# GLU stage of a training step: tile LayerNorms one iteration later, tile 1 transposed by TensorE, w_down's transposes copied by halves

## The chip, the cores and the metric

One NeuronCore of a Trainium2 chip runs the whole program in one launch. The metric is device time in microseconds (us) of one execution, the median of several runs. A profiled execution gives, besides its time, a trace of every instruction. Engines: PE is TensorE, PEld its weight load, DVE VectorE, ACT ScalarE, POOL GpSimd, SP SyncE, which here only issues DMAs.

## The reference

The kernel computes a transformer block with modulation from a condition vector c, and the gradients of its eleven inputs: `x` (2048 rows of 512), a memory of 8 rows, Wq, Wk, Wv, Wo (32 heads of 128), w_gate, w_up (512 x 1792), w_down (1792 x 512), c and w_mod. All inputs and outputs are bf16. The changed part is the GLU half:

```python
h = _layernorm(x, axis=-1) * (1 + ca) + sa
x = x + ga * _A_ref(h, A_mem0, A_Wq, A_Wk, A_Wv, A_Wo, A_seg_len)   # recurrent attention, 64 segments of 32 rows
h = _layernorm(x, axis=-1) * (1 + cb) + sb
g = jnp.einsum('bsd,df->bsf', h, w_gate)
u = jnp.einsum('bsd,df->bsf', h, w_up)
x = x + gb * jnp.einsum('bsf,fd->bsd', _sigmoid(g) * u, w_down)
```

with `_vjp(grad_out)` of all of it after that.

## The kernel before

The program has four big stages: the attention forward (`phase2`, one iteration for each of 64 segments), the GLU forward and backward (`phase3`), the attention backward, and the remaining weight gradients. The change is in `phase3`, and in one line of `phase2`'s last segment.

`phase3` works through 16 tiles j of 128 rows in a software pipeline of seven steps (`run_pipeline`, L2100). In iteration it, step k works on tile it - k, and the deepest step comes first: s6, s5, ..., s0, and then `after(it)`. The steps are:

- s0 (L1141): issues the loads of tile j+1 on SP (`glu_load`, L1066: x, four DMAs from AOA, dout) and does the LayerNorm of tile j: t0 and x1 (L1150, L1152), statistics on DVE (L1154 to L1158), rstd on POOL (L1161), xhf on DVE (L1165), xh2, a bf16 copy of xhf, on ACT (L1166), h2a and h2 (L1168, L1170) and db = dout * gb (L1173) on DVE; h2 and db are stored from POOL (L1171, L1174). For tile 0 all of this was done within the attention stage.
- s1 (L1178): hdT, the transposes of h2 and db, by two DMA transposes issued by SP (L1183, L1184). Tile 0 has its hdT already.
- s2 (L1194): gate and up on PE, four chunks of 448 columns, alternately (L1205, L1209), with eight evictions on ACT: sg = sigmoid(gate) (L1206) and u (L1210, through the helper at L61). It appends `out`, which makes hh and umh on DVE (L1213, L1215), to the list `late`.
- s3 (L1221): hhT by a DMA transpose (L1225); dU = (db w_down^T) * sg: PE with w_downT (L1232), eviction with the product on DVE (L1234); then `flush()` runs what is in `late`, and dg on DVE (L1236).
- s4 (L1242): the product with w_down (L1247), duT and dgT by DMA transposes (L1250, L1251), b_bf on ACT (L1253).
- s5 (L1266): dh (L1272) with w_upT and w_gateT, and the LayerNorm's backward on DVE and ACT.
- s6 (L1313): sums of rows by PE (L1315), the transpose of da (L1319).

So in a steady iteration PE runs s6, s5, s4, s3, s2 without a break, and the LayerNorm of tile `it` follows the DVE work of s5 and s3.

The weights have to be transposed once: w_downT (`wdT_piece`, L1120: for each of four column blocks c two groups of seven PE transposes into the PSUM tile tp, the first group copied by DVE, the second by ACT), and w_gateT, w_upT (`wT_piece`, L1107, groups of eight, copied by ACT). `turns` (L1130) says in which iteration's `after` they run: w_downT and the first two groups of w_gate in iteration 2, the rest in 3 and 4. The tp tiles have two buffers (`psT`, L1090) and the mm tiles of all products five (`psM`, L1089). hdT, h2, db and sg have two buffers each; u, umh, hhT, duT and dgT one.

The order of instructions on each engine comes from a scheduler, with parts pinned to the program's order: PE and ACT up to the end of iteration 2 (L1352), DVE over the stage (L1374). Each engine then executes its queue strictly in that order, and a waiting instruction holds all behind it. That holds for SP and its DMAs too. A DMA also waits for the landing of the eighth DMA before it on its issuer, whose semaphore it uses again.

In the last attention segment `turn_p` (L872) transposes ET on PE and writes Pst: a copy of 32 rows (L874) and a product with rden (L875), both on DVE, three times.

Of the kernel before, what the change touches and what calls it, by code (L numbers as in the profile page):

```python
# [9 lines left out]
AF = mybir.ActivationFunctionType  # L10
# [30 lines left out]
class K:  # L41
# [395 lines left out]
    def phase2(self):  # L437
        nc, tc, cfg, io = self.nc, self.tc, self.cfg, self.io
        D, DC, H, E, L, M, T, G, NS = cfg.D, cfg.DC, cfg.H, cfg.E, cfg.L, cfg.M, cfg.T, cfg.G, cfg.NS
        GW = 128  # L440
        NP = 3
        PG = 4
# [10 lines left out]
        with ExitStack() as ctx:  # L453
# [39 lines left out]
            NT = cfg.NT  # L493
# [148 lines left out]
            first = b_pieces(0)  # L642
# [160 lines left out]
            for s in range(NS):  # L803
                s4 = s % nseg_t
# [66 lines left out]

                def turn_p(pi):  # L872
                    ps, n = transposes_part(ET, pi)
                    nc.vector.tensor_copy(Pst[96:128, pi * PG:pi * PG + n, :], ps[96:128])  # L874
                    nc.vector.tensor_tensor(Pst[0:120, pi * PG:pi * PG + n, :], ps[0:120],  # L875
                                            rden[:, pi * PG:pi * PG + n].unsqueeze(2).to_broadcast([120, n, 128]), op=ALU.mult)

# [79 lines left out]
                Pst = sb2.tile([128, G, 128], BF16, name="Pst", bufs=1)  # L957
# [119 lines left out]
    def phase3(self):  # L1077
        nc, tc, cfg, io = self.nc, self.tc, self.cfg, self.io
        D, DC, F, FC, NT, T = cfg.D, cfg.DC, cfg.F, cfg.FC, cfg.NT, cfg.T
# [7 lines left out]
        with ExitStack() as ctx:  # L1087
# [5 lines left out]
            w_gate, w_up, w_down, w_gateT, w_upT = self.w_gate, self.w_up, self.w_down, self.w_gateT, self.w_upT  # L1093
            w_downT = wtp.tile([128, DC, F], BF16, name="w_downT")
# [6 lines left out]
            def tp8():  # L1101
                return psT.tile([128, 8, 128], BF16, name="tp", tag="t")
# [4 lines left out]
            def wT_piece(src, dst, fc0, n, k):  # L1107
                def f():
                    for fc in range(fc0, fc0 + n, 2):
                        m = min(2, fc0 + n - fc)  # L1110
                        tp = tp8()
                        for i in range(m):
                            for c in range(DC):
                                nc.tensor.transpose(tp[:, i * DC + c, :], src[:, c, (fc + i) * 128:(fc + i + 1) * 128],
                                                    self.ident[:])
                        self.evac("act" if k is None or (fc // 2 + k) % 2 else "dve", dst[:, fc:fc + m, :],
                                  tp[:, 0:m * DC, :].rearrange("p (i c) d -> p i (c d)", i=m))
                return f

            def wdT_piece(c):  # L1120
                def f():
                    for f0 in range(0, FC, 7):
                        tp = tp8()
                        for i in range(7):
                            nc.tensor.transpose(tp[:, i, :], w_down[:, f0 + i, c * 128:(c + 1) * 128], self.ident[:])
                        self.evac("act" if f0 else "dve", w_downT[:, c, f0 * 128:(f0 + 7) * 128],
                                  tp[:, 0:7, :].rearrange("p i f -> p (i f)"))
                return f

            turns = {2: [wdT_piece(c) for c in range(DC)] + [wT_piece(w_gate, w_gateT, 0, 4, None)],  # L1130
                     3: [wT_piece(w_gate, w_gateT, 4, 10, None), wT_piece(w_up, w_upT, 0, 4, None)],
                     4: [wT_piece(w_up, w_upT, 4, 10, None)]}

# [2 lines left out]
            def load(j):  # L1136
                if j >= NT or j in ins:
                    return
                ins[j] = self.glu_first.get(j) or self.glu_load(j, nc.sync)

            def s0(j):  # L1141
                r0, r1 = j * 128, (j + 1) * 128
                load(j + 1)
                st = ins.pop(j)
                if j == 0:
                    st.update(x1=self.first_x1, rstd=self.first_st[:, 9:10], xh2=self.first_xh2)
                    return st
                a_rows = st["a_rows"]
                t0 = sbp.tile([128, D], F32, name="t0", tag="f32tmp", bufs=5)
                nc.vector.tensor_tensor(t0[:], a_rows[:], ga_bc[:], op=ALU.mult)  # L1150
                x1 = sbp.tile([128, D], F32, name="x1", bufs=4)
                nc.vector.tensor_tensor(x1[:], t0[:], st["x0"][:], op=ALU.add)  # L1152
                sts = sbp.tile([128, 6], F32, name="st", bufs=2)
                nc.vector.bn_stats(sts[:], x1[:])  # L1154
                mv = sbp.tile([128, 2], F32, name="mv", bufs=2)
                nc.vector.bn_aggr(mv[:], sts[:])
                ve = sbp.tile([128, 1], F32, name="ve3", bufs=2)
                nc.vector.tensor_scalar_add(ve[:], mv[:, 1:2], EPS)  # L1158
                rstd = sbp.tile([128, 1], F32, name="rstd2", bufs=6)
                i0 = len(self.traced())  # L1160
                nc.gpsimd.tensor_tensor(rstd[:], ve[:], mhalf[:], op=ALU.pow)  # L1161
                self.pin(i0, [mybir.EngineType.Pool])
                xh2 = sbp.tile([128, D], BF16, name="xh2", bufs=5)
                xhf = sbp.tile([128, D], F32, name="xhf", tag="f32tmp", bufs=5)
                nc.vector.tensor_scalar(xhf[:], x1[:], mv[:, 0:1], rstd[:, 0:1], op0=ALU.subtract, op1=ALU.mult)  # L1165
                nc.scalar.activation(xh2[:], xhf[:], AF.Copy)  # L1166
                h2a = sbp.tile([128, D], F32, name="h2a", tag="f32tmp", bufs=5)
                nc.vector.tensor_tensor(h2a[:], xhf[:], cb1_bc[:], op=ALU.mult)  # L1168
                h2 = sbp.tile([128, D], BF16, name="h2", bufs=2)
                nc.vector.tensor_tensor(h2[:], h2a[:], sb_bc[:], op=ALU.add)  # L1170
                nc.gpsimd.dma_start(self.H2ROWS[r0:r1, :], h2[:])  # L1171
                db = sbp.tile([128, D], BF16, name="db", bufs=2)
                nc.vector.tensor_tensor(db[:], st["dout"][:], gb_bc[:], op=ALU.mult)  # L1173
                nc.gpsimd.dma_start(self.DBROWS[r0:r1, :], db[:])  # L1174
                st.update(db=db, x1=x1, rstd=rstd, xh2=xh2, h2=h2)
                return st

            def s1(j, st):  # L1178
                if j == 0:
                    st["hdT"] = self.first_hdT  # L1180
                    return st
                hdT = sbp.tile([128, 2 * DC, 128], BF16, name="hdT", bufs=2)
                nc.sync.dma_start(hdT[:, 0:DC, :], st["h2"][:], transpose=True)  # L1183
                nc.sync.dma_start(hdT[:, DC:2 * DC, :], st["db"][:], transpose=True)  # L1184
                st["hdT"] = hdT
                return st
# [7 lines left out]
            def s2(j, st):  # L1194
                r0, r1 = j * 128, (j + 1) * 128
                hdT = st["hdT"]
                sg = sbp.tile([128, F], BF16, name="sg", bufs=2)
                u = sbp.tile([128, F], BF16, name="u", bufs=1)
                hh = sbp.tile([128, F], BF16, name="hh", bufs=2)
                umh = sbp.tile([128, F], BF16, name="umh", bufs=1)  # L1200
                for ch in range(NCH):
                    sl = slice(ch * CH, (ch + 1) * CH)
                    gp = mm()
                    for c in range(DC):
                        nc.tensor.matmul(gp[:, 0:CH], lhsT=hdT[:, c, :], rhs=w_gate[:, c, sl], start=(c == 0), stop=(c == DC - 1))  # L1205
                    nc.scalar.activation(sg[:, sl], gp[:, 0:CH], AF.Sigmoid)  # L1206
                    up = mm()
                    for c in range(DC):
                        nc.tensor.matmul(up[:, 0:CH], lhsT=hdT[:, c, :], rhs=w_up[:, c, sl], start=(c == 0), stop=(c == DC - 1))  # L1209
                    self.evac("act", u[:, sl], up[:, 0:CH])  # L1210

                def out():
                    nc.vector.tensor_tensor(hh[:], sg[:], u[:], op=ALU.mult)  # L1213
                    nc.gpsimd.dma_start(self.HHROWS[r0:r1, :], hh[:])
                    nc.vector.tensor_tensor(umh[:], u[:], hh[:], op=ALU.subtract)  # L1215

                late.append(out)
                st.update(sg=sg, hh=hh, umh=umh)
                return st

            def s3(j, st):  # L1221
# [148 lines left out]
                if it >= 5:  # L1370
                    later(it)

            self.run_pipeline(NT, [s0, s1, s2, s3, s4, s5, s6], deepest_first=True, after=after)
            self.pin(i0, [ET.DVE])  # L1374
            self.pin_behind(i0, self.pinned, [ET.PE, ET.DVE, ET.Activation, ET.Pool, ET.SP])
            accs = self.flat(self.Wk, 2 * DC * F, 2 * D, F32)
# [7 lines left out]
        with ExitStack() as ctx:  # L1384
# [36 lines left out]
            for (rows, outw) in ((self.DGROWS, io["out_7"]), (self.DUROWS, io["out_8"])):  # L1421
                for ch in range(NCH):
                    xr = xrs.pop(0)
                    for c in range(DC):
                        ps = psG.tile([128, CH], F32, name="gps", tag="g")
# [864 lines left out]
```

## Time and profile before

| | us |
|---|---|
| time before, median of three runs (lowest, highest) | 3062.4 (3058.02, 3064.0) |
| profiled execution, own time | 3064.78 |
| its span (mean granted clock of TensorE) | 3063.0 (0.991) |
| PE busy in the span | 2975.5 |
| GLU's first gate matmul starts | 976.89 |
| stretch 976 to 1034: PE busy, granted clock | 46.76 of 58, 0.94 |
| stretch 1034 to 1284: PE busy, granted clock | 250.00 of 250, 1.00 |

Times inside the profile count from the start of the span. A line of the view of waits reads: who waited, for whom, us in total, times, longest. A line of a timeline reads: start, duration, engine, line of the kernel, operation, out<-in, partitions x elements; an x and a number at its end say how many like instructions were merged; in brackets stands the idle time of the engine before it, and what ended it. A line of the windows view gives, for a stretch, its length, the busy time of PE, PEld, DVE, ACT and POOL with the number of instructions, the granted clock of TensorE (1.00 is full), the mean busy share of the DMA engines and GB/s. Some tiles live in memory of the attention weights, whose names the profile shows: Wk is w_gate and w_up (as source), Wq is hdT of tile 0 (under L1205, L1209, L1232) and w_gateT, w_upT, Wv is w_down.

### The profile page before, as it was taken

The numbers are of one execution on the slowest core, as the hardware profiler recorded it, in microseconds if no ns is written. First come the engines' busy times: TensorE is split into PE (matmuls) and PEld (weight loads), VectorE is DVE, ScalarE is ACT, GpSimd is POOL, SyncE is SP. The second block draws the span as 40 slices with busy tenths as digits, with TensorE's granted clock in tenths as the row PEclk, the third lists the DMA queues.
The fourth block names the chain that finished last, engine by engine and source line by source line (L and its number), as shares of the span: only waits on it lengthen the run. The fifth ranks groups of instructions, "written<-read, shape, count | busy, mean of one in ns | idle before, by whom it ended". The sixth has DMA issues, their size and how long they took to land. (4 is left out here: it accounts for less than half of the span.)

```text
span 3063.0 us, 106593 instructions
## 1 busy us (share of the span) xinstructions
PE 2975.5 (97%) x44297; PEld 1859.8 (61%) x44297; DVE 1605.9 (52%) x3744; ACT 1288.2 (42%) x3182; POOL 1220.6 (40%) x2645
## 2 busy tenths in 40 slices
PE   6999999999998999989899999999999999999999
PEld 3666666666665544445567777777777754445454
DVE  5566566656656788732255555555555632322230
ACT  2555565555554533321255555555555520101011
POOL 2555555555554222211344444444444422333321
PEclk8999999999999999999999999999999999999999
DMA  9888888888888899987499999999999997666574
GB/s 307 217 219 209 216 220 205 219 215 210 217 215 265 199 230 229 239 254 246 155 248 248 245 246 243 247 246 253 248 239 248 246 284 265 214 193 220 182 247 140
DMA packets 838567, 703.54 MB, mean 230 GB/s; under 512 B 538722, under 2 KB 711042, under 8 KB 837188
## 3 DMA queue, kind: packets, MB, share of 16 engines
q1 hardware_dynamic: 712916, 486.69, 64.3%
q0 software_dynamic: 54512, 148.63, 15.3%
q10 hardware_dynamic: 70656, 61.41, 6.4%
q8 instruction: 348, 5.70, 0.8%
q14 instruction: 135, 1.11, 0.1%
HBM read 295.19 MB, written 276.35 MB: 187 GB/s over the span
## 5 line engine op out<-in xcount | busy, mean ns | idle before, releaser
L2080 PE MATMUL gps<-rows,hrows 128*128 128x512 bf16 (+2 forms) x2160 | 417.5, 355 | 0.0
L2080 PEld LDWEIGHTS <-hrows 128*128 128x128 bf16 x2160 | 211.3, 98 | 204.5
L63 DVE CAST ot<-gps 128x512 bf16<-128x512 f32 (+3 forms) x76 | 48.2, 634 | 294.7 <-PE gps L2080 208.4
L1786 POOL COPY dOst<-RAd 96x512 bf16<-96x512 bf16 x128 | 75.1, 611 | 307.6 <-DVE RAd L63 307.3
L61 ACT ACTIVATE ot<-gps 128x512 bf16<-128x512 f32 (+3 forms) x75 | 41.3, 551 | 359.9 <-PE gps L2080 214.7
L658 PE MATMUL pass_ps<-Wv,hT 128*32 128x512 bf16 (+2 forms) x2304 | 188.2, 357 | 0.0
L2084 POOL DMA_DIRECT2D out_dram<-ot x108 | 81.4, 753 | 260.3 <-DVE ot L63 132.7
L1034 POOL TENSOR_TENSOR Pst<-Pst,rden 120x1408 bf16<-120x1408 bf16 x63 | 159.8, 2536 | 56.7 <-issue 35.3
L255 PEld LDWEIGHTS <-hT 128*32 128x32 bf16 x4096 | 125.1, 97 | 94.2 <-DMA Wq<-in_A_Wq_dram 4.6
L61 ACT ACTIVATE dVT<-g_ps 128x480 bf16<-128x480 f32 (+1 forms) x192 | 104.7, 545 | 97.8 <-PE g_ps L1742 97.4
L63 DVE CAST Vst<-pass_ps 96x512 bf16<-96x512 f32 x128 | 87.3, 682 | 106.4 <-ACT RBv L61 101.3
L215 PE MATMUL dh_ps<-WvT,dVT 128*32 128x512 bf16 x2048 | 134.3, 382 | 0.1
L2094 PE MATMUL gps5o<-WoT,rows 128*128 128x512 bf16 x592 | 128.4, 379 | 1.8 <-DMA rows<-OSR 1.8
L255 PE MATMUL pass_ps<-Wq,hT 128*32 128x512 bf16 x2048 | 125.6, 383 | 4.5 <-DMA Wq<-in_A_Wq_dram 4.5
L223 PE MATMUL at_ps<-Wo,OT 128*32 128x256 bf16 x4096 | 124.6, 274 | 2.8 <-DMA Wo<-in_A_Wo_dram 2.4
L658 PE MATMUL pass_ps<-Wv,hb 128*32 128x512 bf16 (+2 forms) x636 | 127.2, 345 | 0.0
L255 PE MATMUL pass_ps<-Wk,hT 128*32 128x512 bf16 x2048 | 124.8, 381 | 1.8 <-POOL hT L547 1.1
L255 PE MATMUL pass_ps<-WoT,dyT 128*32 128x256 bf16 (+1 forms) x3072 | 122.7, 308 | 0.9 <-ACT dyT L1860 0.9
L223 PE MATMUL dhq_ps<-WqT,dQT 128*32 128x256 bf16 x4096 | 122.9, 273 | 0.0
L793 POOL DMA_DIRECT2D Vst<-RBv x192 | 99.2, 522 | 58.6 <-ACT ET L840 38.3
L215 PE MATMUL dh_ps<-WkT,dKT 128*32 128x512 bf16 x2048 | 122.3, 380 | 0.0
L223 PEld LDWEIGHTS <-dQT 128*32 128x32 bf16 x4096 | 109.8, 97 | 15.6
(448 smaller groups left out, 7007.5 us busy)
## 6 DMA issues: line engine op xcount, KB each, us to landing
OSR<-Ost SPq DMA_DIRECT2D x64, 352.0 KB
OT<-OT SPq DMA_DIRECT2D x64, 352.0 KB
VT<-VTr SPq DMA_DIRECT2D x64, 352.0 KB
PS<-Pst SPq DMA_DIRECT2D x64, 352.0 KB
OT_l<-OT SPq DMA_DIRECT2D x64, 352.0 KB
Pst_l<-PS SPq DMA_DIRECT2D x64, 352.0 KB
VT_l<-VT SPq DMA_DIRECT2D x64, 352.0 KB
DVR<-rows_x POOLq DMA_DIRECT2D x64, 352.0 KB, 6.2
```

Of the source, the lines that this page charges most:

```text
L61: return nc.scalar.activation(out, in_, AF.Copy)
L63: return nc.vector.tensor_copy(out, in_)
L215: self.nc.tensor.matmul(ps[32 * j:32 * j + 32, :], lhsT=lhsT, rhs=w, start=(n < 4), stop=(n >= total - 4), tile_position=(0, 32 * j))
L223: nc.tensor.matmul(ps[32 * j:32 * j + 32, :], lhsT=x[k], rhs=w[k][:, 256 * d:256 * d + 256], start=(n == 0), stop=(n == total - 1), tile_p ...
L255: self.nc.tensor.matmul(ps[32 * j:32 * j + 32, :], lhsT=lhs(c), rhs=rhs, start=(c == 0), stop=(c == DC - 1), tile_position=(0, 32 * j))
L658: nc.tensor.matmul(ps[32 * j:32 * j + 32, o * E:(o + n) * E], lhsT=lhsT, rhs=wc[:, 3 * a + hl:3 * (a + n - 1) + hl + 1:3, :], start=(c == ...
L793: nc.gpsimd.dma_start(Vst[96 + 8 * j:104 + 8 * j, :], rb[32 * j + o:32 * j + o + 8, :])
L1034: nc.gpsimd.tensor_tensor(Pst[0:120, :, :], Pst[0:120, :, :], rden[:, :].unsqueeze(2).to_broadcast([120, G, 128]), op=ALU.mult)
L1786: nc.gpsimd.tensor_copy(dOst[0:96, 512 * hf:512 * hf + 512], RAd[0:96, 512 * hf:512 * hf + 512])
L2080: nc.tensor.matmul(ps[:, 0:ng * E], lhsT=hrows[:, tp_, c * 128:(c + 1) * 128], rhs=rows[:, tp_, 0:ng * E], start=(tp_ == 0), stop=(tp_ == ...
L2084: nc.gpsimd.dma_start(outw[c * 128:(c + 1) * 128, h0:h0 + 3 * (ng - 1) + 1:3, :], ot[:, 0:ng * E].rearrange("p (h e) -> p h e", e=E))
L2094: nc.tensor.matmul(pss[gg][:], lhsT=src[0][:, src[1], gg * E:(gg + 1) * E], rhs=dyrows[:, tp_, :], start=(tp_ == order[0]), stop=(tp_ == o ...
```

## The change

Five edits:

1. For tiles from 2 on, s0 is run at the start of s1: the LayerNorm of tile j moves from iteration j to iteration j+1. There it comes behind s3 of tile j-2, and its own hdT transposes follow at once. Tiles 0 and 1 stay.
2. Tile 1's xh2 is copied by POOL and not by ACT.
3. Tile 1's hdT is made by eight PE transposes into one tp tile and one ACT copy, and not by two DMA transposes.
4. w_downT's transposes run inside s2 of tile 0 (ahead of s1 in iteration 2), ordered by halves: first the four groups of the first seven chunks, copied by ACT, then the four of the second, copied by DVE.
5. In `turn_p` the copy of 32 rows moves from DVE to ACT.

```diff
                     ps, n = transposes_part(ET, pi)
-                    nc.vector.tensor_copy(Pst[96:128, pi * PG:pi * PG + n, :], ps[96:128])
+                    nc.scalar.activation(Pst[96:128, pi * PG:pi * PG + n, :], ps[96:128], AF.Copy)
...
-            def wdT_piece(c):
-                def f():
-                    for f0 in range(0, FC, 7):
+            def wdT_pieces():
+                for f0 in range(0, FC, 7):
+                    for c in range(DC):
                         tp = tp8()
                         for i in range(7):
                             nc.tensor.transpose(tp[:, i, :], w_down[:, f0 + i, c * 128:(c + 1) * 128], self.ident[:])
-                        self.evac("act" if f0 else "dve", w_downT[:, c, f0 * 128:(f0 + 7) * 128],
+                        self.evac("dve" if f0 else "act", w_downT[:, c, f0 * 128:(f0 + 7) * 128],
                                   tp[:, 0:7, :].rearrange("p i f -> p (i f)"))
-                return f
-
-            turns = {2: [wdT_piece(c) for c in range(DC)] + [wT_piece(w_gate, w_gateT, 0, 4, None)],
+
+            turns = {2: [wT_piece(w_gate, w_gateT, 0, 4, None)],
...
-                nc.scalar.activation(xh2[:], xhf[:], AF.Copy)
+                if j == 1:
+                    nc.gpsimd.tensor_copy(xh2[:], xhf[:])
+                else:
+                    nc.scalar.activation(xh2[:], xhf[:], AF.Copy)
...
                 hdT = sbp.tile([128, 2 * DC, 128], BF16, name="hdT", bufs=2)
+                if j == 1:
+                    tp = tp8()
+                    for i in range(2 * DC):
+                        src = st["h2"] if i < DC else st["db"]
+                        nc.tensor.transpose(tp[:, i, :], src[:, (i % DC) * 128:(i % DC) * 128 + 128], self.ident[:])
+                    nc.scalar.activation(hdT[:], tp[:], AF.Copy)
+                    st["hdT"] = hdT
+                    return st
...
                 st.update(sg=sg, hh=hh, umh=umh)
+                if j == 0:
+                    wdT_pieces()
                 return st
...
-            self.run_pipeline(NT, [s0, s1, s2, s3, s4, s5, s6], deepest_first=True, after=after)
+            first = lambda j: s0(j) if j < 2 else None
+            second = lambda j, st: s1(j, st if j < 2 else s0(j))
+            self.run_pipeline(NT, [first, second, s2, s3, s4, s5, s6], deepest_first=True, after=after)
```

As the scheduler places them, in the changed program: on PE the first three w_down groups follow tile 0's gate and up, and the other five, tile 1's eight transposes and the two first w_gate groups alternate with dU's matmuls of tile 0; on ACT the four w_downT copies follow u of tile 0, then come hdT of tile 1 and two w_gateT copies, and xh2 of tile 2 stands ahead of the last u of tile 1; on SP hhT, duT and dgT of tile 0 come ahead of hdT of tile 2, and in each later iteration hdT comes ahead of duT, dgT and hhT, where it stood behind them.

## The prediction

> **What bounds the kernel now.** I read the page's busy times first, then the PE's waits in the stage that is edited (976 to 1034 us of the span), then its windows, then the timelines of ACT and PE there.
>
> ```profile
> PE 2975.5 (97%) x44297; PEld 1859.8 (61%) x44297; DVE 1605.9 (52%) x3744; ACT 1288.2 (42%) x3182; POOL 1220.6 (40%) x2645
> ```
>
> PE is busy for 97% of the span: time is won only where PE waits or runs slowly. The view of who waited for whom, for PE from 976 to 1034 us, lists us in total, times, longest:
>
> ```profile
> PE mm L1209 <- ACT sg L1206: 4.2, 1, 4.2
> PE mm L1247 <- DMA hhT<-hh: 2.0, 1, 2.0
> PE tp L1114 <- ACT Wq L61: 1.9, 1, 1.9
> PE tp L1125 <- ACT w_downT L61: 1.7, 1, 1.7
> PE tp L1125 <- DVE w_downT L63: 0.6, 1, 0.6
> ```
>
> The windows view (PE, PEld, DVE, ACT, POOL busy; granted clock; DMA share; GB/s) shows a second loss, the clock:
>
> ```profile
> 981.80:985.20 3.40, 0.15 (x1) 0.10 (x1) 2.50 (x6) 1.27 (x3) 1.18 (x3) 1.00 0.65 189
> 985.20:988.60 3.40, 3.40 (x10) 1.37 (x9) 2.88 (x6) 2.45 (x6) 1.14 (x2) 0.50 0.57 174
> 988.60:992.00 3.40, 1.67 (x23) 1.35 (x22) 2.62 (x6) 2.05 (x4) 0.66 (x2) 1.00 0.56 150
> 1005.70:1009.10 3.40, 1.44 (x18) 0.91 (x16) 3.33 (x5) 2.87 (x5) 1.65 (x3) 1.00 1.05 267
> 1009.10:1012.50 3.40, 3.40 (x24) 2.28 (x22) 0.29 (x1) 1.88 (x2) 0.00 (x1) 0.50 1.16 134
> 1028.00:1284.00 256.00, 255.76 (x1344) 123.48 (x1344) 210.45 (x384) 101.20 (x175) 61.98 (x114) 1.00 0.95 223
> ```
>
> Twice a stretch with little PE work is followed by 3.4 us at half clock. The last row is the steady loop: PE has no gap at all, so nothing can be won there, only lost. All the gain has to come from the ramp before 1028. Where the 4.2 us come from stands in ACT's timeline (start, us, ..., idle before):
>
> ```profile
> 983.93 0.63 ACT L1166 ACTIVATE xh<-xhf 128x512 bf16<-128x512 f32 x1 [9.70 <-DVE xhf L1165]
> 984.47 0.53 ACT L1206 ACTIVATE sg<-mm 128x448 bf16<-128x448 f32 x1
> 984.89 0.54 ACT L61 ACTIVATE u<-mm 128x448 bf16<-128x448 f32 x1
> ```
>
> xh of tile 1 stands ahead of tile 0's first sigmoid on ACT and waits for DVE's LayerNorm. PE fills its five buffers and stops. PE's timeline gives the marks that I sum between:
>
> ```profile
> 985.05 1.55 PE L1209 MATMUL mm<-Wk,Wq 128*128 128x448 bf16 x4 [4.21 <-ACT sg L1206]
> 989.00 0.94 PE L1125 MATMUL tp<-ident,Wv 128*128 128x128 bf16 x14
> 999.23 0.92 PE L1205 MATMUL mm<-Wk,hdT 128*128 128x448 bf16 x4
> 1008.30 0.82 PE L1247 MATMUL mm<-Wv,hhT 128*128 128x512 bf16 x3 [1.96 <-DMA hhT<-hh]
> 1015.40 3.19 PE L1232 MATMUL mm<-w_downT,hdT 128*128 128x448 bf16 x16
> ```
>
> **Part 1: xh of tile 1 goes to POOL; ACT is free for the sigmoids.** Removed from ACT: one copy of 0.63 us with its 9.70 us of idle. What is late next? The built program keeps the old waits of the first sg and the first u: they write memory that the last attention segment's VTr and Ost held, so they wait for the stores VT<-VTr (issued 974.63) and OSR<-Ost (976.06). The trace has these landing at 980.84 and 981.96, long before 984.47, so they were hidden. Now they are the bound. I take sg at 980.95 and u at 982.05. After u, ACT issues one eviction per 0.43 us (984.47 to 984.89). PE's group of four costs 0.757 (977.65 to 978.40). PE's fifth group ends at 980.7 at the latest; the sixth needs sg's buffer (981.55 to 982.3), the seventh u's (982.65 to 983.4), the eighth ends at 984.2. Before, the w_down turns began at 989.00: **4.8 us earlier**. Of that 2.5 to 2.9 is the earlier ACT, the rest the half clock (groups of 1.55 and 1.70 us instead of 0.92).
>
> The clock: a 1.44 us busy window was followed by 0.50, one of 1.67 by 1.00. The new window 978.4 to 981.8 holds some 2.4 us of PE work. I take no slow window; bound 0 to 1.7 us (half of 3.4). The Trainium skill, "TensorE: Matmul & The Clock Gate", Part 1, puts half rate after at least one idle window of about 3.4 us; by it the sum would be the same, but the row of 1.44 us shows that a window need not be empty, and the measurement decides.
>
> On POOL the copy costs about 0.62 (its 128x512 copies of L752 at 970.07), at 983.9, ahead of the store of h2, which waits until 985.35 anyway: nothing. The Trainium skill, "GPSIMD Engine Reference", Key points, speaks against this: POOL shares its SBUF interfaces with VectorE and contends with DVE instructions of two SBUF inputs, and h2a at 983.93 is one. If both stretched, LayerNorm of tile 1 would end later than 985.96, yet DVE is first needed at 988.2 (below): 2.2 us of cover, so zero by either.
>
> **Part 2: LayerNorm of tile 2 leaves the ramp; w_down by halves.** Nine DVE instructions (986.37 to 992.2) stood before DVE's w_downT copies, and ACT's second xh (990.18) before ACT's. Both go. The order is now four copies on ACT (0.92 each, one per 0.83 back to back), then four on DVE (0.62). With two tp buffers, I go through PE's new order: tp1, tp2 by 985.0; ACT copies 985.05 to 988.5 behind the last u; tp3 when tp1 is out (986.0), tp4 986.9, tp5 987.7, tp6 988.55, tp7 and tp8 989.0 to 990.15 against DVE's copies 988.2 to 990.85; dU's matmuls of tile 0 fit in the gaps. Part 3 adds eight transposes of tile 1 (0.45 us, as L1114's eight at 997.46 to 997.90) and one ACT copy 128x1024 of 1.0 us, in place of two DMA transposes: PE 990.35, ACT 990.9 to 991.9; the two w_gate turns, the last four dU matmuls, and tile 1's gate starts at 993.2. This stretch lasts 9.0 us against 10.2 (989.00 to 999.23): **1.2 us**. Without the free DVE, tp5 to tp8 would cost it back.
>
> **Part 3: to dU of tile 1 (before 999.23 to 1015.40, 16.2 us).** Gate and up of tile 1 take 6.05, to 999.25. hhT of tile 0 waited behind two hdT transposes and the loads (issued 1001.01, landed 1008.25). Now it has no transposes ahead and hh is ready at 992.0: issue about 993.6, landing 4 to 7.2 us later, at most 1000.8; PE wants it at 1000.2 and can use it until 1001.5. That wait goes, and the second half-clock window with it. What is late next is ACT: xh of tile 2 now lies on it behind DVE (hh, umh 2.2, du 2.3, dg 1.1, LayerNorm to xhf 3.8 from 990.85: 1000.1), then u, then seven copies of w_gate and w_up of 0.93: the last tp is free at 1005.7, dU of tile 1 starts at 1006.9. 13.7 us: **2.5 us**.
>
> hdT of tile 2 is now behind duT and dgT of tile 0 on SP (4.1 and 3.8 us of issue, rows at 1003.54 and 1007.75): issue 1004.3 to 1007.0, landing 2.6 to 4 us later, 1008 to 1011; PE wants it at 1009.9. Up to a microsecond late, but the next wait of 1.9 us (L1114 for ACT, itself set by DVE) hides that. I take nothing, bound 0 to 1.5.
>
> **Part 4: all later tiles.** DVE's order is unchanged but for the tile's number, and SP's transposes move: hdT of a tile now waits for the LayerNorm of the same iteration, and duT, dgT and hhT stand behind it. Steady iteration at 1066.20: db is written at 1070.15, gate and up of that hdT start at 1078.87, 8.7 us. Issue 1.3 and 1.3 to 2.5, landing 2.6 to 6.9 us after issue in all rows: early enough by 1 to 5 us. duT (issued 1069.99, used at 1085.6), dgT (1073.01, 1088.6) and hhT (1076.61, 1091.6) slip by 2.6 us and have 9 and more to spare after landing. In tile 15 the LayerNorm moves to 1252 to 1259, where DVE idled 2.5 and 4.3 us; its hdT is needed at 1266.9. Nothing. The loads of x, AOA and dout go one iteration later together with their tile, so their lead stays one iteration of 18.8 us, and they land 2 to 5 us after issue. POOL's stores of h2 and db of tile 15 end by 1262; they are read back into memory that holds w_gate until 1273.
>
> **Part 5: three Pst copies to ACT.** DVE loses 0.43, 0.43, 0.36; ACT takes about 0.5 each (128x480 at 966.44: 0.47) in its idle 1.84 before 973.64. ao_b_lo then comes 0.6 earlier and so does PE's first gate, which then waits for the stores all the same: nothing; at most 0.5 lost.
>
> **Sum:** 4.8 + 1.2 + 2.5 = 8.5 us. The profiled execution took 3064.8 (span 3063.0): 3056.3. It lies 2.4 above the median of 3062.4, so 3053.9 for a median. About 0.2% (6 us) is what a measurement here can tell from no change.
>
> **Rivals.** A, the stores: VT and OSR took 6.2 and 5.9 us to land, but the QST stores just ahead in their queue 12.6 and 13.4. If the two land 3 us later, or a window falls to half clock after all, part 1 keeps 1 to 2 us, and all 4.5: 3058. For it: DMA share near 1.0 up to 981.8. Against: neither is touched by the change. B, SP's queue: hhT or hdT of tile 2 late by 3 us or more, since transposes took 4 us each in the ramp: gain 5, 3057.5. C, slower: the steady loop gets a wait for hdT. It decides from 8.7 us after db; beyond that each microsecond is paid by 13 tiles. One microsecond: 13 - 8.5 = 4.5 slower, 3067; two, 3080. For it: rows of 6.1 to 6.9 us behind hhT, plus issue of 2.5. Against: hdT now goes out before the other transposes, into the emptiest part of the iteration.
>
> **Chances.** Forecast 0.62; A 0.19; B 0.11; C 0.08. A and B lie mostly within 0.2% (0.26 of their 0.30), the forecast a little (0.02 of it): faster 0.64, within 0.2% 0.28, slower 0.08. Range 3050.5 to 3061: parts 1 to 3 with 2.5 more at best, A and B with their bounds at worst; C is left out.
>
> **What would show it.** Right: PE's wait for sg under 1.6 us and sg at 981; no window at 0.50 before 990; tile 1's gate at 992 to 994; dU of tile 1 at 1006 to 1008; no PE wait for hhT; no gap in the steady loop. Wrong: any PE wait for hdT, sg later than 982.5, or duT or dgT that PE waits for.

## The result, and the profile after

| | before | changed |
|---|---|---|
| median of 22 runs each, us (lowest, highest) | 3059.94 (3053.95, 3064.86) | 3054.16 (3046.44, 3060.67) |
| profiled execution: span, us | 3063.0 | 3050.6 |

The ratio is 0.9981, with an interval of 0.9973 to 0.9988: faster by 3.7 to 8.3 us, 5.8 by the medians, which is 0.19% and clear of no change. A second comparison (8 runs of the changed kernel, 12 of before) gave 0.9974 (0.9964 to 0.9985).

The two spans differ by 12.4 us, more than the medians do, so the first thing is to locate that. I take the same matmuls in both traces, counted from the first gate matmul of the stage (976.89 before, 977.98 after). A second profile of the changed kernel stands beside the first; "sg" is ACT's first sigmoid, "w_down's turns" are the PE transposes of w_down, "acc" is the first L1315 matmul of a tile (L1327 after); with that of tile 0 the steady loop begins, and what lies ahead of it I call the ramp.

| us from the first gate matmul | before | changed | changed, 2nd profile |
|---|---|---|---|
| first sg | 7.58 | 4.25 | 4.99 |
| w_down's turns start | 12.11 | 7.47 | 8.19 |
| gate of tile 1 | 22.34 | 16.58 | 17.30 |
| dU of tile 1 | 38.51 | 30.17 | 34.63 |
| gate of tile 2 | 41.54 | 35.72 | 37.66 |
| acc of tile 0 | 70.51 | 64.68 | 65.87 |
| from there to acc of tile 12 | 225.65 | 225.65 | 225.65 |

So the ramp became 5.8 us shorter (4.6 in the second profile), about as much as the medians differ by; the steady loop is the same to 0.01 us. Of the 12.4 us, minus 1.1 lies ahead of the stage, 5.8 in the ramp, 0.1 from tile 12 to 15 and 7.6 behind the stage's last acc, where both kernels have the same instructions in the same order on every engine. From that acc to the end the changed kernel's two profiles took 1738.0 and 1738.3 us, the kernel before 1745.6, and the other eleven profiles below 1737.3 to 1743.5. The longest of the eleven is e7, the kernel before with one edit, so these profiles do not exclude an effect of the change behind the stage; in the 240 us behind that acc the granted clock is 0.95 in both of these and 0.97 in the changed kernel. I still take most of the 7.6 us for scatter of single executions, because the profiled executions lie apart by that much: that of the kernel before took 3064.78 us, 4.8 above its median, that of the changed kernel 3052.34, 1.8 below its own. That is argued and not shown; the interval of the gain leaves room for some us outside the ramp.

Now the ramp. PE's waits from 977 to 1034 in the changed kernel (the four largest; who waited for whom, us in total, times, longest):

```profile
PE mm L1215 <- DMA hdT<-h: 2.4, 1, 2.4
PE tp L1125 <- ACT w_downT L61: 1.0, 1, 1.0
PE mm L1219 <- ACT sg L1216: 0.9, 1, 0.9
PE tp L1114 <- ACT Wq L61: 0.7, 2, 0.5
```

The 4.2 us for sg are down to 0.9, those for hhT and most of those for ACT are gone; a wait for hdT, which before did not have, is the largest. ACT's timeline shows that the first sg and u are now held by the landing of the stores, as forecast (OSR landed at 983.24; the releaser named for sg is the one the profile infers, VT<-VTr landed at 982.13). In all seven profiles where the first sg comes behind that landing (this one, e1, e7, e8, e10, e11, e12) it starts 0.10 to 0.11 us after it:

```profile
982.23 0.54 ACT L1216 ACTIVATE sg<-mm 128x448 bf16<-128x448 f32 x1 [6.22 <-DMA AOA<-at_rb]
983.34 0.54 ACT L61 ACTIVATE u<-mm 128x448 bf16<-128x448 f32 x1 [0.57 <-DMA OSR<-Ost]
```

PE's timeline has the marks, and the gap of 2.36 us at 1013.70 with matmuls of 1.70 us behind it:

```profile
985.45 0.94 PE L1125 MATMUL tp<-ident,Wv 128*128 128x128 bf16 x14
...
994.56 0.92 PE L1215 MATMUL mm<-Wk,hdT 128*128 128x448 bf16 x4
...
1001.82 1.04 PE L1259 MATMUL mm<-Wv,hhT 128*128 128x512 bf16 x3 [0.15 <-DMA hhT<-hh]
...
1008.15 3.19 PE L1244 MATMUL mm<-w_downT,hdT 128*128 128x448 bf16 x16
1013.70 1.07 PE L1215 MATMUL mm<-Wk,hdT 128*128 128x448 bf16 x4 [2.36 <-DMA hdT<-h]
1014.57 1.70 PE L1219 MATMUL mm<-Wk,hdT 128*128 128x448 bf16 x4
```

The windows view says why they are slow: the window with the wait (1.04 us of PE work) is followed by one at 0.50. The window that I had feared, at 980, stayed at full clock.

```profile
980.20:983.60 3.40, 2.50 (x14) 1.17 (x12) 2.41 (x5) 0.80 (x2) 2.07 (x5) 1.00 1.06 396
...
1011.00:1014.40 3.40, 1.04 (x6) 0.41 (x5) 3.23 (x6) 0.00 (x0) 1.08 (x2) 0.99 1.22 135
1014.40:1017.80 3.40, 3.40 (x11) 1.32 (x9) 2.58 (x6) 1.09 (x3) 1.10 (x2) 0.50 1.06 363
```

And SP's queue (start, us that the issue took) shows what hdT of tile 2 stood behind. h was ready at 1002.79, db at 1003.39; the transpose of h went out at 1007.74 and landed at 1013.65, just ahead of the gate that needs it, that of db went out at 1009.35 and landed at 1014.15:

```profile
995.90 1.96 SPq L1237 DMA_TRANSPOSE hhT<-hh  x1
997.97 4.10 SPq L1262 DMA_TRANSPOSE duT<-du  x1
1002.16 4.17 SPq L1263 DMA_TRANSPOSE dgT<-dg  x1
1006.43 1.22 SPq L1071 DMA_DIRECT2D Wv<-in_A_x_dram  x1
1007.74 1.51 SPq L1193 DMA_TRANSPOSE hdT<-h  x1
1009.35 1.53 SPq L1194 DMA_TRANSPOSE hdT<-db  x1
```

### The profile page after: what moved, and what is told of

It is laid out like the page before. It is cut to its first block, busy times and chain, and to the rows that moved or that the text cites. A ratio compares the mean times of both kernels' runs of the same rounds, so it can differ in the third digit from the quotient of the medians.

```text
span 3050.6 us, 106537 instructions
## 1 busy us (share of the span) xinstructions
PE 2968.0 (97%) x44227; PEld 1858.1 (61%) x44305; DVE 1603.0 (53%) x3741; ACT 1289.5 (42%) x3185; POOL 1221.8 (40%) x2646
## 4 chain that ended last, share of the span: by engine, by line
PE 47%; issue 2%; DMA 1%; POOL 1%; SPq 0%; DVE 0%; ACT 0%; POOLq 0%; DVEq 0%
PE gps L2094 11%; PE dh_ps L215 8%; PE g_ps L1756 6%; PE pass_ps L255 5%; PE gps5o L2108 4%; PE dhq_ps L223 4%; PE dh_tps L215 3%; PE dp_ps L1733 2%; PE tps L1666 2%; PE dp_ps L1741 1%; PE turn_ps L1620 1%; PE dh_ft L323 1%; POOL out_dram L2098 0%; DMA rows<-OSR 0%; PE turn_ps L264 0%
```

## The experiments

The theory: parts 1 to 3 gave what they promised, and hdT of tile 2, queued behind duT and dgT of tile 0, took some of it back. The rivals: the wait is one of landing and not of place; the gain comes from another edit; the chain through ACT absorbs it all anyway. Single runs of one kernel scatter by some 6 us to either side, so the medians (some 11 runs) tell little among variants, and most verdicts rest on the marks of one profile each. The ratio of a run is to executions of the kernel before that were taken with it, whose medians lay from 3059.5 to 3063.9, so compare ratios and not medians. The marks count from the first gate matmul.

| run | median us (runs) | ratio to before | first gate | gate of tile 1 | gate of tile 2 | acc of tile 0 |
|---|---|---|---|---|---|---|
| e1_hdt_first | 3055.77 (12) | 0.9986 (0.9976 to 0.9995) | 978.09 | +17.01 | +33.62 | +61.83 |
| e2_sg_u_memory | 3054.28 (11) | 0.9989 (0.9978 to 1.0) | 983.33 | +14.85 | +32.15 | +59.68 |
| e3_both | 3054.52 (11) | 0.9986 (0.9977 to 0.9996) | 983.72 | +14.85 | +31.47 | +59.68 |
| e4_xh1_on_act | 3058.78 (11) | 1.0003 (0.9995 to 1.0012) | 982.38 | +20.43 | +40.62 | +67.89 |
| e5_wgate_behind_store | 3057.83 (11) | 0.9993 (0.9979 to 1.0007) | 983.24 | +16.54 | +35.09 | +62.37 |
| e6_all_three | 3055.64 (11) | 0.9989 (0.998 to 0.9998) | 982.91 | +16.54 | +33.15 | +61.36 |
| e7_before_xh1_pool | 3059.72 (1) | | 977.17 | +23.42 | +40.34 | +69.31 |
| e8_ln2_early | 3052.87 (1) | | 978.47 | +16.68 | +36.51 | +64.72 |
| e9_loads_after_stores | 3058.74 (12) | 0.999 (0.9978 to 1.0002) | 978.17 | +16.97 | +37.17 | +65.38 |
| e10_pst_on_dve | 3052.9 (1) | | 979.36 | +16.63 | +34.48 | +61.98 |
| e11_hdt1_by_dma | 3060.11 (1) | | 978.19 | +20.61 | +39.45 | +67.66 |
| e12_changed_again | 3053.84 (8) | 0.9974 (0.9964 to 0.9985) | 979.16 | +17.30 | +37.66 | +65.87 |

**e1_hdt_first**: the order on SP alone.

```diff
+                if j == 2:
+                    self.i_hd = len(self.traced())
                 nc.sync.dma_start(hdT[:, 0:DC, :], st["h2"][:], transpose=True)
...
                 nc.sync.dma_start(dgT[:], st["dg"][:], transpose=True)
+                if j == 0:
+                    self.pin(self.i_hd, [mybir.EngineType.SP])
```

> The changed kernel with one difference: on SP the two transposes of hdT of tile 2 are issued ahead of duT and dgT of tile 0 (every other engine keeps its order). All marks count from the first gate matmul of the GLU stage. In the changed kernel gate of tile 2 starts at +35.7 after a wait of 2.36 us for hdT and 3.4 us at half clock, and gate of the last full ramp step, acc of tile 0 (the first L1327 matmul), at +64.7. Theory (queue): hdT is late because it stands behind 8.3 us of issue of duT and dgT. Then it is issued at about +25 (db is written at +25.4), lands by +30, PE has no wait for it, no half-clock window follows, gate of tile 2 starts at +33.2; of the 4.2 us some 1 to 1.5 come back as a wait for ACT at the last w_up turns, so acc of tile 0 starts at about +61.5 (3 us earlier) and the time is about 3 us below the changed kernel's. Rival 1 (landing): the transposes land late whatever their place, because the DMA engines are full there: hdT still lands after +33 and acc of tile 0 moves by less than 1 us. Rival 2 (absorbed, as the prediction had it): the wait goes, but ACT's wait of 1.9 us or more takes its place whole, and acc of tile 0 moves by less than 1 us.

Measured: PE's two largest waits in the ramp, then SP's queue, both of this run.

```profile
PE tp L1114 <- ACT Wq L61: 2.0, 2, 1.1
PE mm L1221 <- ACT sg L1218: 1.3, 1, 1.3
```

```profile
1003.36 1.20 SPq L1195 DMA_TRANSPOSE hdT<-h  x1
1004.65 1.21 SPq L1196 DMA_TRANSPOSE hdT<-db  x1
1005.95 2.46 SPq L1264 DMA_TRANSPOSE duT<-du  x1
1008.46 3.71 SPq L1265 DMA_TRANSPOSE dgT<-dg  x1
```

hdT lands at +28.3 (h) and +31.0 (db), PE does not wait for it, no half-clock window follows in the ramp, and ACT's wait grows from 0.7 to 2.0. Acc of tile 0 is 2.85 us earlier than in the changed kernel's first profile: the queue theory holds. The other profiles agree on the landing: with this order (e1, e3, e6, e9) the half from h lands at +26.1 to +29.8 and PE never waits for it; in the old place (the changed kernel, e2, e4, e5, e10, e12) it lands at +32.1 to +40.6, and PE waits 0 to 3.4 us. They do not agree on the worth: e10, with the old order, has acc of tile 0 at +61.98 (below). So the rival of landing falls; that of absorption falls for the wait of 2.36 us, but not for short waits, as e2 and e3 show next.

**e2_sg_u_memory** and **e3_both**: other addresses for u and sg (an unused tile of 224 bytes, and u ahead of sg); the second also has the order of e1.

```diff
+                if j == 0:
+                    sbp.tile([128, 112], BF16, name="pad", bufs=1)
+                u = sbp.tile([128, F], BF16, name="u", bufs=1)
                 sg = sbp.tile([128, F], BF16, name="sg", bufs=2)
-                u = sbp.tile([128, F], BF16, name="u", bufs=1)
```

> The changed kernel with one difference: u and sg of the GLU stage lie in other SBUF addresses, so that the first sg and u no longer overwrite what the last attention segment still stores (VTr, Ost). The order on every engine is the same. Theory: in the changed kernel the landing of the two stores (+4.15 and +5.26 after the first gate matmul) is what ACT waits for. Then the first sg starts at about +1, PE has no wait for sg, w_down's turns start at +6.1 instead of +7.47 and gate of tile 1 at about +15.2 instead of +16.6. From there little is kept: hhT of tile 0 is issued on SP behind the loads, its landing (+23.8) does not move, and hdT of tile 2 neither; PE waits 1 us or more for hhT and longer for hdT, and acc of tile 0 starts at +64.2 to +64.7 (0 to 0.5 us gained). Rival: the stage is a chain through ACT alone, and the whole 1.4 us arrives at acc of tile 0 (+63.3). Rival 2: the stores were not the bound, sg starts no earlier than +4.

> The changed kernel with both: hdT of tile 2 ahead of duT and dgT of tile 0 on SP, and u and sg in other addresses. Theory: the two add up where hdT no longer holds PE back: gate of tile 1 at +15.2, a wait of 1 us for hhT of tile 0, acc of tile 0 at about +60.8, the time 3 to 4 us below the changed kernel's and 9 to 10 below the kernel before. Rival: the second difference gives nothing beyond the first (acc of tile 0 as in the run with hdT alone, within 0.3 us), since the landing of hhT or DVE sets the end of the ramp. Rival 2: neither helps, about the changed kernel's time.

In both the first sg starts at +0.96, ahead of the landing of VT<-VTr (+1.65 and +1.94), w_down's turns at +6.05 and gate of tile 1 at +14.85: the stores were the bound of part 1, by 1.4 us. What followed was not as I expected: acc of tile 0 came at +59.68, 5.0 earlier, in both. But these two runs reached the first gate matmul 5 us late (see e5), and SP, which does not wait for it, was ahead of the stage: hhT of tile 0 went out at +15.7 and not at +17.9, and hdT landed at +32.1 even in its old place. So what the addresses are worth behind gate of tile 1 can't be read from them. Between the two, the order of e1 saves a wait of 0.5 us for hdT and 0.7 at the gate of tile 2, and nothing at acc of tile 0: ACT's wait is 2.0 with it and 1.3 without. A wait this short is absorbed, as the prediction had it.

**e4_xh1_on_act**: edit 2 undone.

> The changed kernel without its second edit: xh of tile 1 is copied by ACT again, at its old place ahead of tile 0's first sigmoid. Theory (part 1 of the prediction holds): ACT waits until xhf at about +7, sg starts at +7.5 instead of +4.25, PE waits about 4 us for it, a half-clock window follows, w_down's turns start at +11.5 to +12 instead of +7.5, and the loss stays: acc of tile 0 at about +69 (4 to 5 us later), the time 4 to 5 us above the changed kernel's, about 1 us below the kernel before. Rival: what the edit wins at +7.5 is lost again at hdT of tile 2 in the changed kernel, so without it acc of tile 0 moves by less than 2 us.

In PE's waits of this run the sg wait is back, and hdT is late besides:

```profile
PE mm L1216 <- ACT sg L1213: 3.7, 1, 3.7
PE mm L1212 <- DMA hdT<-h: 3.4, 1, 3.4
```

w_down's turns start at +11.63, 4.2 later; gate of tile 1 is 3.9 later, acc of tile 0 3.2. The ratio is 1.0003, the whole gain gone. Part 1 holds; the rival (less than 2 us) falls. This run too reached the first gate matmul late (982.38), so the 3.2 us are the rougher figure.

**e7_before_xh1_pool**: edit 2 alone, on the kernel before.

> The kernel before with the second edit alone: xh of tile 1 copied by POOL. Theory: part 1 of the prediction needs the other edits. The first sg starts at +4.2 to +4.6 after the first gate matmul and w_down's turns at about +7.5 to +8, but the first of each pair of groups is copied by DVE, which still has the LayerNorm of tile 2 ahead of it until about +15.3; PE then waits 5 to 7 us for a tp buffer, and gate of tile 1 starts at +21 to +22.5 (before: +22.3): a gain of 1 us or less. Rival: the edit by itself brings the 4.6 us, gate of tile 1 at about +17.8.

The largest of PE's waits in its ramp:

```profile
PE tp L1125 <- ACT w_downT L61: 6.8, 1, 6.8
```

The turns start at +7.07, 5 us earlier than before, and then stand: ACT's xh of tile 2 waits 5.16 us for DVE and is ahead of ACT's copies, and DVE's first copy (992.40) comes behind the nine LayerNorm instructions. I had named DVE's copy as what PE would wait for; it was ACT's. ACT's timeline of this run:

```profile
990.46 0.63 ACT L1169 ACTIVATE xh<-xhf 128x512 bf16<-128x512 f32 x1 [5.16 <-DVE xhf L1165]
991.00 0.90 ACT L61 ACTIVATE w_downT<-tp 128x896 bf16<-128x896 bf16 x1
```

Gate of tile 1 is 1.1 later than before, acc of tile 0 1.2 earlier. The 4.6 us of part 1 exist only where the copies of w_downT do not stand behind the LayerNorm of tile 2; e8 shows which edit sees to that.

**e8_ln2_early**: edit 1 only from tile 3 on (`j < 2` becomes `j < 3` in `first` and `second`).

> The changed kernel, but the LayerNorm of tile 2 stays in the iteration in which it was before (only tiles from 3 on move). It then stands on DVE behind the w_downT copies and ahead of the evictions of dU of tile 0. Theory: the 5.3 us of nine DVE instructions now hold dU's four PSUM buffers, so PE waits about 3 us in gate and up of tile 1; in return hdT of tile 2 is issued early and is never waited for, and no half-clock window follows. Acc of tile 0 at about +63.5 to +65 (changed kernel +64.7): the move of tile 2's LayerNorm by itself is worth about nothing, because what it wins at dU it loses at hdT. Rival (the prediction's part 2 and 3): without the move both the ramp's DVE wait and a wait of ACT for xh of tile 2 come back, and acc of tile 0 is 2 us or more later than in the changed kernel.

Acc of tile 0 at +64.72 against +64.68: the move of tile 2's LayerNorm by itself is worth nothing, as expected. Gate of tile 1 starts at +16.68, as early as with the move: edit 4, which places the w_downT copies ahead of that LayerNorm, is what cleared the way, and edit 1 was not needed for parts 1 and 2. DVE's timeline of this run, the last copies and the first LayerNorm instruction of tile 2:

```profile
990.97 1.89 DVE L63 COPY w_downT<-tp 128x896 bf16<-128x896 bf16 x3 [0.19 <-PE tp L1125]
992.78 0.68 DVE L1149 TENSOR_TENSOR t<-Wv 128x512 f32<-128x512 bf16 x1
```

hdT lands at +25.4 and is not waited for. The price appears elsewhere than I thought: not at gate and up of tile 1 as a wait for DVE, but at the w_gate turns that the scheduler had put between them, behind the xh of tile 2 on ACT (996.58, after 2.69 us of waiting for DVE); a half-clock window (999.2) follows, which I had excluded. PE's largest wait of this run:

```profile
PE tp L1114 <- ACT Wq L61: 3.6, 3, 2.1
```

**e11_hdt1_by_dma**: edit 3 undone.

> The changed kernel without its third edit: hdT of tile 1 is made by two DMA transposes again. Theory: they stand among the loads on SP and are issued at about +14 to +17, land 4 to 6 us later, so gate of tile 1 starts at +20 to +22 instead of +16.6; hhT of tile 0 goes out 2 to 4 us later behind them and is waited for too; acc of tile 0 at +67 to +70 (changed kernel +64.7). Rival: h and db are ready at +9, the transposes land in time, and without eight PE transposes and a 1.0 us copy on ACT the stage is as fast or 0.5 us faster.

PE's largest wait in the ramp of this run:

```profile
PE mm L1207 <- DMA hdT<-h: 3.9, 1, 3.9
```

The transposes go out at +18.0 and +19.9 and land at +20.6 and +26.2; gate of tile 1 is 4.0 later, acc of tile 0 3.0. By these marks turning tile 1 on PE carries about as much as edit 2 (3.2).

**e10_pst_on_dve**: edit 5 undone, and **e12_changed_again**: the changed kernel itself.

> The changed kernel without its fifth edit: the three Pst copies are on DVE again. From the start of the last output projection (at_ps) to the first gate matmul it takes 10.36 us in the changed kernel, 10.64 before; from there to acc of tile 0 75.0 us in the changed kernel. Theory (part 5: nothing): ao_b_lo comes some 0.3 us later, PE's first gate matmul too (10.6 to 10.9), but sg waits for the landing of the stores in both, so acc of tile 0 is at 74.7 to 75.4 from at_ps. Rival: the 0.3 to 0.6 us of DVE are on the path and arrive at acc of tile 0 (75.6).

> The changed kernel itself once more, for a second profile of it. In its first profile it took 75.04 us from the last output projection (at_ps) to acc of tile 0, with a wait of 2.36 us for hdT of tile 2 and a half-clock window behind it; with the Pst copies on DVE it took 72.62 us, with a wait of 0.6 us for hdT, 1.5 us for hhT and no half-clock window. Theory (scatter of the transposes): the landing of hdT, not the place of the Pst copies, made that difference; the issue of duT and dgT took 8.3 and 7.7 us there. A second profile then lies anywhere from 72.5 to 75.1, with a hdT wait of 0.5 to 2.4 us, and whatever it shows, the sum of the hdT wait and the half clock behind it explains its distance from 72.5 within 0.5 us. Rival: the fifth edit costs 2.4 us by itself; then it is 75.0 again with the Pst wait as the only difference from the other profile.

Without edit 5 the way from the last output projection to the first gate matmul takes 10.64 us, with it 10.36: the 0.3 us are there. But acc of tile 0 came 72.6 us after that projection, outside of both expectations, since PE waited only 0.6 us for hdT of tile 2. The second profile of the changed kernel took 76.2, longer than I allowed for, and by another wait. Its largest PE wait in the ramp, and its windows:

```profile
PE mm L1259 <- DMA hhT<-hh: 3.3, 1, 3.3
```

```profile
979.60:983.00 3.40, 3.40 (x11) 1.40 (x10) 0.00 (x0) 0.00 (x0) 2.59 (x6) 0.50 1.03 383
...
1003.50:1006.90 3.40, 0.08 (x3) 0.01 (x1) 3.33 (x5) 2.66 (x4) 1.43 (x3) 1.00 1.18 260
1006.90:1010.30 3.40, 3.18 (x17) 2.02 (x19) 0.52 (x1) 0.63 (x1) 0.23 (x1) 0.50 1.23 270
```

hhT of tile 0 took 8.4 us to land (5.9 in the first profile), PE waited 3.3 and ran a window at half clock; gate of tile 2 then found hdT there. The sum I had written for this run (hdT's wait and its half clock) fails, because there was no wait for hdT. So the changed kernel has one transpose too late in each profile, now the one, now the other, and what edit 5 does to acc of tile 0 can't be told from that scatter: the rival that it costs 2.4 us is neither shown nor excluded.

**e5_wgate_behind_store**, **e6_all_three**, **e9_loads_after_stores**: a side path, to take the scatter ahead of the stage out, in search of a version that beats both kernels.

```diff
                 if s == NS - 1:
-                    nc.gpsimd.dma_start(self.w_gate, io["B_w_gate"].rearrange("(c p) f -> p c f", p=128))
-                    norms.pop()()
+                    norms.pop()(mid=lambda: nc.sync.dma_start(
+                        self.w_gate, io["B_w_gate"].rearrange("(c p) f -> p c f", p=128)))
...
-                def norm(s=s, Pst=Pst, rden=rden):
+                def norm(s=s, Pst=Pst, rden=rden, mid=None):
...
                     nc.sync.dma_start(self.VT[s], VTr[:])
+                    if mid is not None:
+                        mid()
                     nc.sync.dma_start(self.PS[s], Pst[:])
```

e6 has this, the order of e1 and the addresses of e2; e9 the same, but with the load behind PS<-Pst too.

> The changed kernel with one difference, ahead of the GLU stage: in the last attention segment the load of w_gate (1.8 MB) is issued by SP behind the store VT<-VTr of the segment before, and not by POOL at about the same time. The profiles so far show two cases, whichever GLU variant ran: with the store issued first (956.4, 957.4, 957.5) it lands at 961.5 to 962.8 and the first gate matmul is at 976.9 to 978.1; with the load of w_gate first (store issued 958.3, 959.3, 959.7) the store lands at 967.7 to 968.7, DVE's copies into VTr wait for it, PE waits 2.7 to 3.7 us for rden, runs 3.4 to 6.8 us at half clock, and the first gate matmul is at 982.4 to 983.7. Theory (race): this is a good part of the scatter of single runs. With the fixed order the store lands by 963, PE has no wait for rden there, the first gate matmul is at 978.5 at the latest, and the time is 2 to 3 us below the changed kernel's median (the late case costs 5 and came in 3 of 5 profiles of the changed kernel's variants). Rival: the scatter of the times comes from the stages after (they differed by 4 us too), and the median stays within 1 us; or w_gate then lands too late and the first gate waits.

> The changed kernel with hdT of tile 2 ahead of duT and dgT on SP, u and sg in other addresses, and the load of w_gate behind the store on SP. Theory: with the first gate matmul as early as in the changed kernel's profile (978), the first sg starts at +1, w_down's turns at +6.05, gate of tile 1 at +15, no wait for hdT of tile 2, acc of tile 0 at +60 to +61.5, that is at 1038 to 1039.5 of the span against 1042.7 in the changed kernel, and the time is some 3049 to 3051. Rival: the loads on SP then come later against the stage, PE waits 1 to 3 us for hhT of tile 0, and acc of tile 0 is no earlier than with hdT first alone (+61.8).

> The changed kernel with hdT of tile 2 ahead of duT and dgT on SP, u and sg in other addresses, and the load of w_gate issued by SP behind both stores of segment 62 (VT<-VTr and PS<-Pst), since in the runs with the load between the two the second store landed at 975 and PE waited 2.3 to 2.8 us for Pst. Theory: both stores now land by 968, PE waits for neither rden nor Pst (under 0.5 us each), the first gate matmul is at 977 to 979; w_gate lands at about 973 and w_up at 977, just in time; acc of tile 0 at +59.7 to +61.5, that is 1037 to 1040 of the span, and the median is 3048 to 3051, below the changed kernel's. Rival 1: w_up or w_down now lands late, and PE waits 1 to 3 us for it in tile 0: nothing gained. Rival 2: what is won before the steady loop does not reach the end, because scatter of the later stages (4 us) or a wait there takes it: median within 1.5 us of the changed kernel's 3054.2.

The race is real (last section). But in e5 and e6 the store PS<-Pst then landed at 975 behind the load, PE waited 2.8 and 2.3 us for Pst, and the first gate matmul was as late as in the bad case. In e9 both stores landed by 964.6 and the first gate matmul was at 978.17, as expected; the load itself now held SP (waits of SP's queue in this run):

```profile
SPq L1073 <- DMA Wk<-in_B_w_gate_dram: 8.1, 1, 8.1
```

The eighth DMA behind it had to wait for its landing at 974.7, all that follows on SP went out later (hhT of tile 0 at +21.2 instead of +17.9), and PE waited 3.3 us for hhT. No version of several runs beat the changed kernel in measured time. That e1 to e3 have a ramp 3 to 5 us shorter by their marks, and ratios of 0.9986 and 0.9989 where the changed kernel has 0.9981, stays open: with some 11 runs each the intervals are as wide as that, and e2 and e3 met the late first gate matmul in the profile.

## Why the prediction was right, and where it was wrong

The time came out almost exactly (3053.9 forecast, 3054.16 measured), but by two errors that cancel: the median of before was 3062.4 from three runs and is 3059.94 from 22, and the gain was 5.8 and not 8.5. That is luck. At 0.19% the gain lies on the edge of the 0.2% to which I had given 0.28, against 0.64 for more; and one of the signs that I had named as wrong, a PE wait for hdT, is there.

- **Part 1, forecast 4.8: measured 4.64** (12.11 to 7.47). The landing of the stores sets the first sg and u, as I had it: 982.23 for 980.95, with the whole stage 1.1 us later in this execution; e2 shows the bound by removing it, e4 the value of the edit, e7 and e8 that it needs edit 4. The clock: full in the first profile; in the second a window ran at half clock (979.6), but the turns came 0.72 later because VT<-VTr landed 0.73 later, so the clock cost nothing there. On POOL the copy took 1.13 us and not 0.62, and DVE's h beside it 0.98 and not 0.69; with DVE idle for 2.38 us behind, it cost nothing. The Trainium skill ("GPSIMD Engine Reference", Key points) states that POOL and DVE instructions with two SBUF inputs contend. These two rows agree with it; without them the sum would be the same.
- **Part 2, forecast 1.2: measured 1.12.** The stretch took 9.11 us (9.0 forecast). The reason was half right: the copies had to get past the LayerNorm of tile 2, but edit 4 does that alone (8.9 us in e8, where this LayerNorm has not moved).
- **Part 3, to dU of tile 1, forecast 2.5: measured 2.58** (13.59 us against 13.7). Up to here 8.34 of the 8.5 were won. In the second profile hhT landed later than my limit ("at most 1000.8"), and only 3.9 were won at this mark.
- **The step that failed** is the next sentence of part 3: "Up to a microsecond late, but the next wait of 1.9 us (L1114 for ACT, itself set by DVE) hides that. I take nothing, bound 0 to 1.5." hdT was 2.36 us late, and a half-clock window of 3.4 us followed, which I had not counted behind a wait (1.7 more). ACT's wait did shrink, from 1.92 to 0.20, so 1.7 of it was hidden; 2.5 were lost: 8.34 became 5.83. What was mis-sized was the queue. I gave the two issues ahead of it 4.1 and 3.8 us (4.10 and 4.17 measured), but hhT, the first of the row, went out at 995.90 and not at 993.6 (1.1 of that is the later stage), behind the loads; the load of x took another 1.22; and the landing took 4.8 to 5.9 us, not 2.6 to 4. e1 shows that this place in the queue is the cause.
- **Part 4, nothing: right.** Acc of tile 0 to acc of tile 12 took 225.64 or 225.65 us in every profile, with the old order and the new. Around 1070 the half of hdT from h, which gate and up read, lands at 1068.81 and is used at 1074.12, the other half at 1070.66.
- **Part 5, nothing: right as far as can be seen.** 0.28 us are won ahead of the first gate matmul, where sg waits for the stores anyway; behind it the scatter hides what the edit does.
- **Rivals.** B ("hhT or hdT of tile 2 late by 3 us or more", gain 5) is what happened by mechanism, in the second profile as stated (hhT, a wait of 3.3 us, ramp 4.6 shorter), in the first a little milder (hdT, 2.36 us, 5.8); I had given it 0.11. A did not happen: the stores landed within 0.2 us of their place against the stage in the first profile, 0.9 later in the second. C did not: from tile 3 on hdT keeps at least 4 us in hand in both profiles.

## What to carry to other kernels

When a change shortens a ramp, list what each in-order DMA queue has to issue in it, with issue times and landings, and ask of each transfer whether its place still suits its new due time: here 8.3 us of transposes nobody needed yet stood ahead of one that was due. Count a wait on PE together with the half-clock window that may follow it: one did behind the 2.36 us of the changed kernel, none behind the 3.4 us for hdT in e4. And where single runs scatter by more than the gain, measure the stage by marks within it, and check that the rest of the span is the same work before crediting the change with a difference of spans.

## What the runs showed of the hardware

- **When the clock is halved.** Over the fourteen profiles (behind the first 100 us), each full-clock window of 3.4 us with less than 1.48 us of PE work was followed by one at 0.50 (77 of 77); of those with 1.48 to 2.16 us, 12 of 74; of those with more, none of 11851. The Trainium skill ("TensorE: Matmul & The Clock Gate", Part 1) speaks of an idle window; here a window with up to 1.48 us of work, 43% of its length, was followed by half rate without exception.
- **Two DMA issuers racing.** The store VT<-VTr of segment 62 (SP) landed at 961.3 to 964.2 where it was issued before the load of w_gate (POOL) or at most 0.12 us after it, and at 967.7 to 968.7 where it was 0.42 to 0.84 us after. DVE and PE then stood, here by the timelines of e4, where the store landed at 967.71 (the view names no releaser for DVE):

```profile
967.79 0.76 DVE L63 COPY VTr<-tps 128x512 bf16<-128x512 bf16 x2 [4.15 <-issue]
```

```profile
968.71 0.21 PE L844 MATMUL or_ps<-ones,ET 128*128 128x1 bf16 x3 [3.34 <-DVE rden L849]
```

  With the half clock behind it the first gate matmul came at 982.4 to 983.7, against 976.9 to 979.4 in the rest: in three of the eleven profiles with POOL issuing the load, none of them of the kernel before or the changed one.
- **POOL beside DVE.** A POOL copy of 1.13 us beside two DVE instructions with two inputs: h2a, which had begun 0.03 us earlier, kept its 0.69, the copy took 0.5 longer than POOL's copies of this size at 970.07 before, and h, begun while the copy ran, took 0.98 instead of 0.69. POOL's and DVE's timelines of the changed kernel:

```profile
984.91 1.13 POOL L1166 CAST xh<-xhf 128x512 bf16<-128x512 f32 x1 [0.65 <-DVE xhf L1164]
```

```profile
984.88 0.69 DVE L1170 TENSOR_TENSOR h2a<-xhf,Wv 128x512 f32<-128x512 f32 x1
985.61 0.98 DVE L1172 TENSOR_TENSOR h<-h2a,Wv 128x512 bf16<-128x512 f32 x1
```
